# Fourteen places of their own for the second token weights' tiles, and an earlier start of their loads, in a spectral filter followed by an MLP mixer

## The chip, the cores and the metric

The kernel runs on one core of a Trainium2 chip. The metric is the device time of one execution in microseconds (us), as the median of several runs. The engines are named as in the profile: PE is TensorE (PEld its weight loads), DVE is VectorE, ACT is ScalarE, POOL is GpSimd and SP is SyncE. SP, ACT and POOL also issue DMAs, each in the order of its own instructions; all of them are carried by the same 16 DMA engines.

## The reference

The input has 8 batches of 3008 positions and 256 channels. A spectral filter is applied along the positions, and then an MLP mixer whose first half mixes positions ("token") and whose second half mixes channels:

```
X = np.fft.rfft(x, axis=1)
x = np.fft.irfft(X * (filt_r + 1j * filt_i)[None], n=3008, axis=1)
h = np.maximum(x.transpose(0, 2, 1) @ w_tok1, 0.0) @ w_tok2     # w_tok1 3008x256, w_tok2 256x3008
u = x + h.transpose(0, 2, 1)
out = u + np.maximum(u @ w_ch1, 0.0) @ w_ch2                    # w_ch1 256x1536, w_ch2 1536x256
```

The four mixer weights arrive as 64-bit floats. [...]

## The kernel before

**Two parts.** An opening (up to about 170 us) filters batch 0 and loads and converts all weights; then `mix` walks over 8 batches x 6 column blocks x 6 pairs of channel groups, and the filter of the next batch (`dft` of the next group) is spread between its items.

**The filter of batch 0.** `dft(GROUPS[0])` first transforms 12 pieces of x (`a_unit`, L534) and leaves the result, turned by DVE, in the tile `turned`. Then come 32 steps k. A step has a PE product with the table (`b_unit`, L666: it reads `turned[:, k, :]`), a DVE product with the filter (L671), the PE products back (`bi_unit`, L680), and an ACT copy (L690); after every second step ACT issues a DMA that writes the copies to a DRAM tensor, `g_tmp` (L687). In the same loop POOL loads the filter's rows for later steps (`filt_load`, six DMAs per two steps, L243 to L251), SP loads table pieces (L583), and ACT copies filter rows to the tile's other half (L255). In the last steps and behind the loop, `t4_load` reads `g_tmp` back in another layout (L782): rows of steps 0 to 15 first, then 16 to 23, then 24 to 27, and last those of steps 28 to 31 (six DMAs, three from SP and three from POOL). With these last rows `token_sums` can start (L788, 48 PE products), and then `token_relu` (L864) and the first parts of u (`u_part`, L882 and L874).

**The weights.** A tile of 64-bit weights is brought in and converted in four stages, written as a generator: `begin` issues the DMA into a staging place; `copy` is an ACT instruction that takes the upper words (L283); `middle` is two DVE instructions (L285, L286); `end` is two more (L289, L291), and then either two PE products that add the halves, with an ACT copy out (L329, L330, L332), or DVE additions (L318). The list `tiles` fixes the order: 12 tiles of w_tok1 (`w1_tile`, loaded by SP), 14 of w_tok2 (`w2_load`, L362, loaded by POOL, 470 KB each but 188 KB for the last of each half; the first six go the PE way, the others the DVE way), two of w_ch1 (`wc1_load`, L394, four DMAs of 128 KB each), and the ten of `LAST` (w_ch1 and w_ch2, L394 and L405). Conversion goes at a fixed place of the program: one half tile (a `middle` or an `end`) per filter step, then one tile after another behind the loop, between the token sums and the parts of u, and the rest in the first items of `mix`. For channel tiles POOL forms sums of the weights (`combine`, L382 to L386).

**Where a tile waits and when it is begun.** `stages` lists, in the order of the tiles, the pool and tag of the staging place: 12 times the pool t4, then sixteen places that go round over the two buffers each of u, t and v, then t2 and t3 in turn. So the seventh tile of w_tok2 takes the place of the first one and its DMA waits until DVE has read that. `fill` begins tiles as long as fewer than 5 (for the tiles of `LAST`, 4) lie between the begun and the ended ones; it runs at the end of every conversion, not in the last five filter steps (`pause`), and once more behind the loop, ahead of the last `t4_load`s. `ended` counts program order: a DMA is placed in POOL's queue there, and the queue then goes on by its own waits.

**The region that is shared.** The pool `wcp` has one buffer. Before `mix`, it holds `turned` (columns 0 to 8191 of 32-bit words, 256 for each step) and a small table `wa0` (128 columns more), which is read only by `a_unit`. Behind the filter's loop the same buffer becomes `both`, the channel weights (`chan`, 10,752 columns). The first write into it is the addition L318 of the first channel tile.

Of the kernel before, what the change touches and what calls it, by code (L numbers as in the profile page):

```python
# [10 lines left out]
FP32 = mybir.dt.float32  # L11
I64 = mybir.dt.int64
# [7 lines left out]
N1 = 47  # L20
N2 = 64
NF = N // 2 + 1
D = 256
P = 128
K2 = 32
A = 24
# [14 lines left out]
TC = DT // P  # L41
DC = 1536
JT = DC // P
JP = JT // 2
DH = D // P
# [3 lines left out]
NG = 10  # L49
W2G = -(-N2 // NG)  # L50
# [80 lines left out]
def kernel(  # L131
# [31 lines left out]
    def pool(name, bufs, **kw):  # L163
        return ctx.enter_context(tc.tile_pool(name=name, bufs=bufs, **kw))

    glob = pool("glob", 1)
    wcp = pool("wcp", 1)
# [6 lines left out]
    t4p = pool("t4p", A // TC4 + 1)  # L174
# [36 lines left out]

    w2m = [w2[:, t, 0:7 * 256].rearrange("p (s n) -> p s n", s=7) for t in range(2)]

    turned = wcp.tile([P, K2 * D + P], FP32, tag="wc", name="turned")
    wa0 = turned[:, K2 * D:]
    turned = turned[:, 0:K2 * D].rearrange("p (s d) -> p s d", d=D)
    chan = []


# [46 lines left out]

    early = [(up, "u")] * 2 + [(tp, "t")] * 2 + [(vp, "v")] * 2
    late = [(t2p, "t2"), (t3p, "t3")]
    stages = [(t4p, "t4")] * (A // 2) + (early * 3)[0:TC * W2G + DH] + late * 5

    def stage(n):
        where, tag = stages.pop(0)
        return where.tile([P, n], I64, tag=tag, name="st")

    def halves(st, n, pair):
# [45 lines left out]
    ended = [0]  # L321
# [14 lines left out]
    def w1_tile(i):  # L336
        st = stage(512)
        rows = moe_w_tok1.rearrange("(n2 n1) t -> n2 n1 t", n1=N1)
        q = nc.sync if i < EARLY else nc.gpsimd
        if 2 * i + 2 == A:  # L340
            nc.gpsimd.memset(st.bitcast(U32)[:, 512:1024], 0)
        for j in range(2):
            a = 2 * i + j
            both = a + 1 < A
            src = bass.AP(tensor=rows.tensor, offset=rows.offset + (A - 1 - a) * DT,
                          ap=[[N1 * DT, N2]] + [[(1 + 2 * a) * DT, 2]] * both + [[1, DT]])
            q.dma_start(st[0:P:1 if both else 2, ts(j, DT)], src)
        yield

        h = halves(st, 512, spare_pair())  # L350
        yield next(h)
        yield next(h)
        on_chip(wai_t, *next(h), 512, [(lambda v: v, w1[:, 2 * i:2 * i + 2, :].rearrange("p a t -> p (a t)"))])

    def w2_load(i):

        t, g = divmod(i, W2G)
        nn = min(NG, N2 - g * NG)
        n = nn * N1

        st = stage(512)
        nc.gpsimd.dma_start(st[:, 0:n], moe_w_tok2[ts(t, P), ds(g * NG * N1, n)])  # L362
        yield
        dst = w2[:, t].rearrange("p (a h n2) -> p h n2 a", h=2, n2=HALF)[:, :, ds(g * NG, nn), :]

        def some(h, first, step, w):
            return (lambda v: bass.AP(tensor=v.tensor, offset=v.offset + first, ap=[v.ap[0], [N1, nn], [step, w]]),
                    dst[:, h, :, 0:w])

        parts = [some(0, A - 1, -1, A), some(1, A, 1, A - 1)]  # L370
        if i < BY_PE:
            h = halves(st, n, spare_pair())
            yield next(h)
            yield next(h)
            on_chip(ident, *next(h), n, parts)
        else:
            yield from rounded(st, n, parts, False)
# [12 lines left out]
    def wc1_load(i, late=True):  # L390
        c, q = divmod(i, DC // 512)
        st = stage(512)
        for g in range(CB):
            nc.gpsimd.dma_start(st[ts(g, CW)], moe_w_ch1[ds((g * DH + c) * CW, CW), ts(q, 512)])  # L394
        yield

        yield from rounded(st, 512, [(lambda v: v.rearrange("p (i j n) -> p i j n", j=2, n=P),
                           chan[0][:, 2 * q:2 * q + 2, slice(0, 5, 4) if c == 0 else slice(1, 7, 5)])], late)
        if c == DH - 1 and 2 * q >= PLAIN:
            combine(chan[0][:, 2 * q:2 * q + 1])  # L400
            put_off.append(2 * q + 1)

    def wc2_load(i):
# [11 lines left out]
        while put_off:  # L415
# [4 lines left out]
    LAST = ((wc2_load, 0), (wc1_load, 1), (wc1_load, 4), (wc2_load, 1), (wc1_load, 2), (wc2_load, 2), (wc1_load, 5),  # L420
            (wc2_load, 3), (wc2_load, 4), (wc2_load, 5))

    tiles = ([w1_tile(i) for i in range(A // 2)] + [w2_load(i) for i in range(TC * W2G)]
             + [wc1_load(c * (DC // 512), False) for c in range(DH)] + [f(i) for f, i in LAST])
# [20 lines left out]
    def convert_end(copy_now=True):  # L445
        ended[0] += 1
        advance(end)
        if copy_now:
            copies()
        fill(5)  # L450
# [9 lines left out]
    begun, pause = [0], []  # L460

    def fill(ahead):
        while not pause and begun[0] < len(tiles) and begun[0] < ended[0] + (4 if begun[0] >= len(tiles) - len(LAST) else ahead):
            start()

    def start():
        advance(begin)
        begun[0] += 1
# [3 lines left out]
    xs, ahead = {}, []  # L472
# [304 lines left out]
    t4 = {}  # L777
# [481 lines left out]
    with tc.manual_schedule():  # L1259
# [36 lines left out]
        pause.clear()  # L1296

        fill(5)
        for c in range(A // TC4):
            t4_load(0, c, PARTS[3], P, (nc.sync, nc.gpsimd)[c % 2])  # L1300
# [27 lines left out]
        n = MT * JP  # L1328
# [58 lines left out]
```

## Time and profile before

| what | value |
|---|---|
| runs shown | 2398.6, 2398.96, 2395.35 us (median 2398.6) |
| the profiled execution | 2395.43 us, its span from first to last instruction 2393.7 us |
| TensorE's granted clock | 0.996 of full speed over the span |
| PE busy 0 to 100 / 100 to 200 / 200 to 300 / 300 to 400 us | 82.52 / 93.88 / 96.20 / 100.00 us |
| the filter's steps | L666 begins at 31.44 us, the last L680 ends at about 102.7 us |
| last write of g_tmp (L687), and POOL's read behind it (L782) | issued at 104.39 us and 108.88 us |
| token sums (L788) | begin at 111.00 us |
| DMAs of w_tok2 (L362) | fourteen, issued from 65.1 to 113.7 us; to landing 4.1 / 6.9 / 10.1 us (least, median, most) |
| DMA over the span | 294.28 MB, 123 GB/s on average; 210 to 283 GB/s between 60 and 106 us |

A row of a timeline has the start, the duration, the engine, the line, the operation with its output and input, and in brackets the idle time before it with what ended it. A row of waits has the engine, its line and tile, what it waited for, and then the total in us, the number of times and the longest. A row of stretches has the stretch and its length, each engine's busy time with the number of instructions, the granted clock, the busy share of the DMA engines and what they moved in GB/s; since transfers overlap, the share can be over 1.

### The profile page before, as it was taken

To read this page: it belongs to the slowest core of one execution; us is meant where nothing else is said; L and a number is where in the kernel's file an instruction comes from. 1 tells how busy PE (TensorE), PEld (TensorE's weight loads), DVE (VectorE), ACT (ScalarE), POOL (GpSimd) and SP (SyncE) were. 2 spreads that over 40 slices of the span, in tenths; PEclk is the share of its full clock that TensorE was granted. 3 is DMA by queue.
4 is the path that set the end of the run, shared out by engine and by line. 5 is a ranking of instruction groups with operands and counts; after the bars stand their busy time and mean duration, and the time that the engine had idled before them with its cause. 6 is when DMAs were issued, how large, how long until landed. Compare 5 with 4: busy or idle time off the path is not lost.

```text
span 2393.7 us, 36991 instructions
## 1 busy us (share of the span) xinstructions
PE 2356.6 (98%) x13108; PEld 2007.5 (84%) x13108; DVE 1943.6 (81%) x3653; ACT 688.1 (29%) x1339; POOL 641.0 (27%) x1124
## 2 busy tenths in 40 slices
PE   7999999999999999999999999999999999999998
PEld 4667789888898888988888888988889888898887
DVE  7797887888887888878887788788888788877776
ACT  5732222322223222232222222132222322212222
POOL 8485533211211121222111211221121112112121
PEclk8999999999999999999999999999999999999999
DMA  8864446333354333533344333533335433331100
GB/s 228 235 197 134 146 129 223 112 108 94 112 178 134 94 96 110 198 112 95 104 154 153 107 94 104 193 113 108 94 112 177 135 94 97 108 130 33 38 15 21
DMA packets 190423, 294.28 MB, mean 123 GB/s; under 512 B 34444, under 2 KB 124962, under 8 KB 190238
## 3 DMA queue, kind: packets, MB, share of 16 engines
q1 hardware_dynamic: 148750, 231.24, 31.1%
q0 software_dynamic: 34688, 53.83, 8.6%
q10 hardware_dynamic: 6800, 6.85, 0.9%
q8 instruction: 104, 1.70, 0.3%
q14 instruction: 81, 0.66, 0.1%
HBM read 209.06 MB, written 82.72 MB: 122 GB/s over the span
## 4 chain that ended last, share of the span: by engine, by line
PE 93%; DVE 3%; DMA 2%; issue 1%; POOL 1%; ACT 0%; SPq 0%; DVEq 0%; ACTq 0%; POOLq 0%
PE ps_po L1022 35%; PE ps_pg L975 20%; PE ps_pg L1004 15%; PE ps_b L527 3%; PE ps_b L839 3%; PE ps_acc L896 3%; PE ps_pg L527 2%; PE ps_acc L839 2%; PE ps_b L896 2%; PE ps_acc L874 2%; PE ps_b L874 2%; DVE t L953 1%; PE ps_pg L666 1%; DMA x<-in_x_dram 1%; PE ps_b L680 1%
## 5 line engine op out<-in xcount | busy, mean ns | idle before, releaser
L1030 POOL DMA_DIRECT2D out_dram<-r x752 | 408.3, 551 | 1452.1 <-issue 864.0
L1009 ACT ACTIVATE hh<-hh 128x512 f32<-128x512 f32 (+1 forms) x568 | 342.7, 621 | 989.1 <-DVE hh L953 989.1
L953 DVE TENSOR_TENSOR hh<-ps_pg,s 128x512 f32<-128x512 f32 (+3 forms) x852 | 475.4, 585 | 167.2 <-ACT s L978 157.1
L1022 PE MATMUL ps_po<-t,wc 128*128 128x256 f32 (+1 forms) x2296 | 556.4, 379 | 0.8 <-DVE t L953 0.8
L1022 PEld LDWEIGHTS ps_po<-t,wc 128*128 128x128 f32 x2296 | 427.1, 190 | 93.0 <-issue 33.9
L1022 PE MATMUL ps_po<-hh,wc 128*128 128x256 f32 (+1 forms) x1722 | 411.5, 375 | 1.1 <-POOL wc L386 1.1
L975 PE MATMUL ps_pg<-v,wc 128*128 128x256 f32 (+1 forms) x1704 | 406.6, 375 | 0.0
L1022 PEld LDWEIGHTS ps_po<-hh,wc 128*128 128x128 f32 x1722 | 326.8, 190 | 40.2 <-POOL wc L386 1.9
L975 PEld LDWEIGHTS ps_pg<-v,wc 128*128 128x128 f32 x1704 | 323.5, 190 | 36.9 <-DVE v L953 0.4
L1004 PE MATMUL ps_pg<-u,wc 128*128 128x256 f32 (+1 forms) x1136 | 287.7, 376 | 3.3 <-DVE hh L953 3.1
L953 DVE TENSOR_TENSOR t<-t,hh 128x256 f32<-128x256 f32 (+1 forms) x576 | 247.6, 430 | 19.8
L1004 PEld LDWEIGHTS ps_pg<-u,wc 128*128 128x128 f32 x1136 | 213.9, 190 | 32.7 <-DVE hh L953 7.5
L953 DVE TENSOR_TENSOR s<-ps_pg,hh 128x512 f32<-128x512 f32 (+1 forms) x284 | 193.3, 681 | 29.6
L978 ACT COPY s<-ps_pg 128x256 f32<-128x256 f32 (+1 forms) x284 | 104.4, 367 | 326.5 <-PE ps_pg L975 326.4
L953 DVE TENSOR_TENSOR t<-hh 128x512 f32<-128x512 f32 (+1 forms) x288 | 194.4, 675 | 0.6 <-ACT hh L1009 0.6
L975 PE MATMUL ps_pg<-u,wc 128*128 128x256 f32 (+1 forms) x568 | 166.9, 375 | 0.4 <-DVE hh L953 0.4
L1004 PE MATMUL ps_pg<-v,wc 128*128 128x256 f32 (+1 forms) x568 | 166.4, 375 | 0.0
L975 PEld LDWEIGHTS ps_pg<-u,wc 128*128 128x128 f32 x568 | 106.3, 190 | 14.1 <-DVE hh L953 2.1
L1004 PEld LDWEIGHTS ps_pg<-v,wc 128*128 128x128 f32 x568 | 107.3, 190 | 12.7
L953 DVE TENSOR_TENSOR u<-ps_acc,u 128x256 f32<-128x256 f32 (+1 forms) x84 | 46.1, 549 | 72.4 <-PE ps_acc L896 50.2
L953 DVE TENSOR_TENSOR u<-ps_b,u 128x512 f32<-128x512 f32 (+2 forms) x126 | 74.5, 591 | 28.9 <-PE ps_b L896 26.7
L896 PE MATMUL ps_acc<-w 128*128 128x256 f32 (+1 forms) x336 | 85.2, 376 | 0.0
(168 smaller groups left out, 2708.4 us busy)
## 6 DMA issues: line engine op xcount, KB each, us to landing
w<-w_tmp SPq DMA_DIRECT2D x84, 448.0 KB
w<-w_tmp SPq DMA_DIRECT2D x35, 896.0 KB
out_dram<-r POOLq DMA_DIRECT2D x696, 32.0 KB, 3.5
g_tmp<-t SPq DMA_DIRECT2D x112, 192.0 KB
t<-g_tmp SPq DMA_DIRECT2D x42, 512.0 KB
t<-z_tmp SPq DMA_DIRECT2D x196, 96.0 KB
z_tmp<-t SPq DMA_DIRECT2D x72, 256.0 KB
wb<-wbi_t SPq DMA_DIRECT2D x56, 256.0 KB
```

Of the source, the lines that this page charges most:

```text
L527: nc.tensor.matmul(outs(i, j), stat(i, j), mov(i, j), start=True, stop=True)
L666: nc.tensor.matmul(ps, wbs[k // WC][:, 0:2 * P:2, k % WC], turned[:, k, :].unsqueeze(1), start=True, stop=True)
L839: nc.tensor.matmul(ps[:, at], w[:, n], mov, start=(j == 0 and i in (0, 2)), stop=(j == AP - 1 and i >= 5))
L874: nc.tensor.matmul(ps[:, ds(q * P, n)], t4[b, c][:, r, ts(dh, P)], wai[:, 0:n], start=(first and q == 0), stop=(not first and q == 3))
L896: nc.tensor.matmul(ps[:, ds(j * hw, hw)], h1[:, n, :], w2m[m % 2][:, at, 0:hw], start=(i < 2 and j == 0), stop=(j == len(todo) - 1))
L953: nc.vector.tensor_tensor(out=out, in0=in0, in1=in1, op=op)
L975: nc.tensor.matmul(ps[:, 0:hw], chan[0][:, jp, n, :], mov, start=True, stop=True)
L978: nc.scalar.copy(out=s[:, 0], in_=g[0][:, 0, 0:hw])
L1004: nc.tensor.matmul(ps[:, 0:hw], chan[0][:, jp, n, :], mov, start=True, stop=True)
L1009: nc.scalar.activation(out=hs, in_=hs, func=AF.Relu)
L1022: nc.tensor.matmul(po[i][:, j, 0:hw], chan[1][:, jp, n, :], mov, start=(jp == 0 and first == 1), stop=(jp == JP - 1 and last == 1))
L1030: q.dma_start(bass.AP(tensor=ob.tensor, offset=ob.offset + row * D + g * cw, ap=[[N1 * D, 32], [D if h else -D, n], [1, cw]]), blocks[ts(g ...
```

## The change

The buffer of `wcp` gets the name `early_wc` and its full width from the start. Twelve w_tok1 tiles keep their places. The fourteen w_tok2 tiles get a place each: the six buffers of u, t and v; three behind `wa0` (from column 8320 on, 940 columns apart); and five in the columns of `turned` (0, 1024, 2048, 3072, 4096; each the columns of four steps). An exchange in the list gives the narrow last tile of the first half the last, short piece. The two first w_ch1 tiles take the buffers of u (before: of t). From the twelfth tile on, `fill` may run 5 tiles ahead of the ended ones and one more for every two tiles ended beyond two, up to 11; the tiles of `LAST` stay at 4. The order of the conversions is the same.

```diff
-    turned = wcp.tile([P, K2 * D + P], FP32, tag="wc", name="turned")
-    wa0 = turned[:, K2 * D:]
-    turned = turned[:, 0:K2 * D].rearrange("p (s d) -> p s d", d=D)
+    early_wc = wcp.tile([P, 2 * JP * 7 * P], FP32, tag="wc", name="turned")
+    wa0 = early_wc[:, K2 * D:K2 * D + P]
+    turned = early_wc[:, 0:K2 * D].rearrange("p (s d) -> p s d", d=D)
...
-    stages = [(t4p, "t4")] * (A // 2) + (early * 3)[0:TC * W2G + DH] + late * 5
+    stages = [(t4p, "t4")] * (A // 2) + early + [(early_wc, K2 * D + P + n * NG * N1) for n in (0, 2, 4)]
+    stages += [(early_wc, n * 4 * D) for n in range(5)] + early[0:DH] + late * 5
+    stages[A // 2 + W2G - 1], stages[A // 2 + 8] = stages[A // 2 + 8], stages[A // 2 + W2G - 1]
 
     def stage(n):
         where, tag = stages.pop(0)
+        if where is early_wc:
+            return where[:, ds(tag, min(2 * n, 2 * JP * 7 * P - tag))].bitcast(I64)
         return where.tile([P, n], I64, tag=tag, name="st")
...
     def fill(ahead):
-        while not pause and begun[0] < len(tiles) and begun[0] < ended[0] + (4 if begun[0] >= len(tiles) - len(LAST) else ahead):
+        while not pause and begun[0] < len(tiles):
+            if begun[0] >= len(tiles) - len(LAST):
+                ahead = 4
+            elif begun[0] >= A // 2:
+                ahead = 5 + min(max(ended[0] - 2, 0) // 2, 6)
+            if begun[0] >= ended[0] + ahead:
+                break
             start()
```

## The prediction

> **What bounds the kernel now.** I read the engines' busy time first, then TensorE's waits, then tables of stretches over the start.
>
> The page's first part:
>
> ```profile
> PE 2356.6 (98%) x13108; PEld 2007.5 (84%) x13108; DVE 1943.6 (81%) x3653; ACT 688.1 (29%) x1339; POOL 641.0 (27%) x1124
> ```
>
> TensorE (PE) is idle for only 2393.7 - 2356.6 = 37 us. The table in steps of 100 us puts 17.5 us of it before 100 us, 6.1 between 100 and 200, 3.8 between 200 and 300, and almost none from there to 2300 us. So the bound is TensorE, and only the opening can move: a microsecond won or lost before about 260 us moves the end by a microsecond. The change acts between 60 and 170 us. TensorE's waits from 111 us to 262 us:
>
> ```profile
> PE ps_pg L1004 <- DVE hh L953: 3.1, 3, 2.7
> PE ps_b L788 <- DMA t<-g_tmp: 2.1, 1, 2.1
> PE ps_po L1022 <- POOL wc L386: 1.1, 2, 0.6
> PE ps_po L1022 <- DVE t L953: 0.8, 3, 0.4
> PE ps_acc L882 <- ACT h L864: 0.7, 1, 0.7
> PE ps_pg L975 <- DVE hh L953: 0.4, 1, 0.4
> ```
>
> No row names the weight loads that the change moves. The second does matter: L788, the first batch's token sums, starts at 111.00 us, when the filter's result has been written to DRAM (g_tmp) and read back. Next, who waited between 96 and 131 us:
>
> ```profile
> POOL t L782 <- DMA g_tmp<-t: 10.1, 1, 10.1
> ...
> ACT both L283 <- DMA st<-in_moe_w_tok_dram: 6.4, 2, 5.6
> ```
>
> ScalarE (ACT) waits 5.6 us for a second-token-weight load (call these tiles w2 0 to 13), because GpSimd's (POOL's) queue held five of them for 10.1 us behind the reads of g_tmp. VectorE (DVE) then waits too; from its timeline:
>
> ```profile
> 116.59 0.41 DVE L285 TENSOR_SCALAR both<-both 128x470 uint32<-128x470 uint32 x1 [2.46 <-ACT both L283]
> ```
>
> Last, the stretches; the last two columns are the busy share of the 16 DMA engines and GB/s:
>
> ```profile
> 60.00:70.00 10.00, 10.00 (x40) 7.75 (x39) 7.90 (x15) 8.84 (x16) 8.90 (x17) 1.00 0.72 210
> 70.00:80.00 10.00, 10.00 (x39) 7.73 (x39) 7.76 (x15) 8.86 (x17) 8.12 (x16) 1.00 0.87 238
> 80.00:90.00 10.00, 10.00 (x36) 7.16 (x35) 6.95 (x13) 9.01 (x16) 4.48 (x9) 1.00 1.05 239
> 90.00:98.00 8.00, 7.97 (x31) 6.23 (x30) 6.13 (x12) 7.10 (x15) 0.54 (x1) 1.00 0.87 283
> 98.00:106.00 8.00, 6.61 (x21) 3.66 (x19) 5.97 (x12) 6.21 (x14) 0.54 (x1) 1.00 0.97 232
> 106.00:110.00 4.00, 2.63 (x6) 1.00 (x6) 2.88 (x8) 2.44 (x6) 1.02 (x3) 1.00 0.28 83
> ```
>
> The DMA engines are nearly full from 60 to 106 us and then almost free for 4 us. In those 4 us the last write of g_tmp (issued at 104.39, landed at 108.30) and its first read (108.37 to 110.86) take place.
>
> **The change part by part.**
>
> *What it moves.* Before, w2 0 to 5 are issued from 65.1 to 85.7 us, w2 6, 7 and 8 at 89.3, 93.5 and 98.3 (each waiting for its place), w2 9 to 13 from 110.6 to 113.7 and the first channel tile at 119.2 to 123.5. After, all fourteen have places that need no wait: u, t, v and the tail of the region are free, and its columns are read for the last time by step 19, before 75 us. By the new allowance two loads come at step 13 (about 61 us) and eleven by step 25; the last three and the channel tile (into u, free at 88.7 us) follow at once. All stand ahead of POOL's reads of g_tmp.
>
> *Issue.* Each load costs POOL the same 0.55 us as before. Five come earlier within the filter's loop, and POOL idles 0.5 to 0.7 us per two steps there, so I cost them at nothing; the filter's loads behind them are needed 15 us later by step count and land in 2 to 7.5 us. If that cover fails, ACT's copy L255 waits.
>
> *The gain.* VectorE's 2.46 us go. Its conversions run one after another at 2.94 us (starts at 119.53, 122.51, 125.44), so all later ones come up to 2.46 us earlier, until VectorE meets what TensorE paces: v at 140.91 needs ACT's u (done at 138.75, lead 2.1), t at 150.09 needs hh (done at about 149.2, lead 0.9). A lead of 0.9 removes TensorE's 0.16 at 150.8 and 0.55 at 158.1, and most of 0.57 at 167.1, whose POOL L386 follows VectorE's L318: 0.9 to 1.3, I take 1.1. Ends: 0 (a later load is late instead) and 2.5 (the whole lead). The 2.7 us at 210.9 stay: they end a chain of DMAs from TensorE's own unit at 183.6, which moves along.
>
> *The cost.* The loads keep their bytes; they now lie ahead of the transfers that start L788. What one occupies: the five issued at 110.55 to 112.19 and 113.66 land 5.3, 6.2, 7.5, 10.1 and 9.5 us later; the first and third are (119.15 - 115.85) / 2 = 1.65 us apart per 470 KB. Pulled ahead of 106 us are four such (6.6), the 188 KB one (0.66) and 512 KB of channel weights (1.8): 9.1 us of DMA time. Free before 106 us by the table: 2.8 + 1.3 + 0 + 1.0 + 0.2 = 5.4 us (one minus the share, times the length). If all of it can be filled, 9.1 - 5.4 = 3.7 us are left when the last write is issued; if half, 6.4. Transfers land about in the order in which they were issued, whichever queue they came by: w2 8, issued on POOL's queue at 98.27, takes 8.5 us to 106.8, and reads of 64 KB issued by SyncE (SP) at 99.1 and 99.7 land at 107.0 and 107.2. So what is left delays the last write, its read and L788. No trace of before has this load at this place: ends 0 and 6.4, and I take 5.0, the middle of 3.7 and 6.4.
>
> A rule speaks against that order. The Trainium skill (DMA: Bandwidth & Descriptors, Queues, rings and completion order) says that each DMA engine takes the queues in turn, packet by packet, so that SP's reads would not stand behind POOL's backlog. The landings at 107 us do not show it. By the rule the sum would be about 0 (second rival).
>
> *Places shared with a live tile.* The filter's steps 20 to 31 still read the region's other columns. Waits go by the columns touched: TensorE's second unit loads weights from this tile at 6.03 us, while the first unit's copy into other columns runs only at 7.12. So nothing (third rival otherwise).
>
> *Sum.* +5.0 - 1.1 = +3.9 us on the profiled execution's 2395.43, that is 2399.3. The runs shown spread: 2395.35, 2398.6 and 2398.96, and with the profiled one their mean is 2397.1. I predict 2397.1 + 3.9 = 2401.0. A measurement of this kernel tells 0.2% (4.8 us) from no change, so this lies within it.
>
> **The rivals.**
>
> *ACT is held too (slower).* ACT's write of steps 28 and 29 was ready at 101.2 us and issued at 102.01: the copy behind it waits 1.2 us for a read of g_tmp, issued by SP at 97.1, to land (101.9), since they share a completion semaphore. If such reads land 10 us after issue, as w2 5 did (85.67, 9.7 us), that is 107: ACT stalls about 5 us, and the last steps' copies and the last write follow it. Then the write is issued near 109.4, and 3.9 + 2.5 us of write and read come on top: L788 near 117.4, +6.4, net +5.3 or 2402.4. It decides once the reads of 96.3 to 98.5 land later than about 104. For it: the 9.7 us, and 8.1 us for the read of 98.53. Against: POOL itself is held by its own semaphores at 80 to 86 us (waits of 0.3 to 0.9), which thins its backlog.
>
> *The queues share.* If each queue gets its turn at the engines, the last write and first read wait only about as long again as they occupy them: between 95 and 111 us queue q10 takes 14.6% of 16 us for three writes (0.8 each), q1 34.8% for eighteen transfers (0.3): 1.1 us. With the gain: 0, or 2397.1. Against: the landings at 107 us. (This is where the rule above would lead.) If moreover w2 8's absence after 98 us frees ACT's 1.2 us and VectorE's lead counts whole, -3.7, or 2393.4.
>
> *Waits go by the whole tile.* Then step 24's matmul (about 84 us) waits for w2 9, loaded just before it: 10 us, as the 9.7 above, so 2407. Against: 6.03 before 7.12.
>
> *The change doesn't bring the loads forward*, because POOL is held. Then 0, as for sharing queues.
>
> **How the numbers follow.** Forecast 0.48; ACT held 0.27; queues share, or loads not forward 0.17; gain only 0.05; whole tile 0.03. Slower by over 0.2% (+4.8): all of the whole tile, three quarters of ACT held (0.20), a quarter of the forecast, whose own span is 3.7 - 1.1 to 6.4 - 1.1, or +2.6 to +5.3 (0.12): 0.35. Faster by over 0.2% needs more than the gain rival offers, but for the spread of runs: 0.05. The rest, 0.60, is within. The range goes from 2393.5 (gain only) to 2405.0 (ACT held at 2402.4, with the runs' own 1.9 above their mean); the whole tile is left out.
>
> **What would show it.** Gain: ACT's 5.6 us wait for w2 and VectorE's 2.46 are gone, and POOL L386 no longer holds TensorE at 158 and 167. Cost: L788 starts near 116 us, not 111.0; the DMA share between 106 and 110 us is near 1; w2 loads issued about 90 us land more than 8 us later. ACT held: its wait for a read of g_tmp is well over 1.2 us. If L788 starts at or before 111 us, my order of landings or the free time is wrong, and the kernel is up to a few us faster; if TensorE waits in the filter's loop (L666, L680), a cover failed and it is slower than I say.

## The result and the profile after

The changed kernel takes 2403.7 us (median of 9 runs, 2401.68 to 2406.36), the kernel before, beside it, 2396.42 us (9 runs, 2394.95 to 2398.96). The ratio is 1.0032, with an interval of 1.0023 to 1.004: slower by 7.3 us. The profiled execution took 2404.92 us with a span of 2403.1, which is 9.4 us more than the span before. The change made the kernel slower, as forecast, and the time lies in the forecast range (2393.5 to 2405.0), but above the forecast of 2401.0: +3.9 us was forecast, and slower by more than 0.2% (4.8 us) had a chance of 0.35.

Busy time, the page's first part, of the kernel after:

```profile
PE 2361.8 (98%) x13108; PEld 2011.7 (84%) x13108; DVE 1943.0 (81%) x3653; ACT 688.7 (29%) x1339; POOL 641.6 (27%) x1124
```

TensorE has the same 13108 matmuls, but is busy 5.2 us longer with them. It is no new work, so its matmuls were slower somewhere. The rest of the 9.4 us, 4.2, is idle time. TensorE's waits from 111 to 271 us:

```profile
PE ps_b L798 <- DMA t<-g_tmp: 5.2, 1, 5.2
PE ps_pg L1014 <- DVE hh L963: 3.8, 2, 2.8
PE ps_po L334 <- DVE both L295: 2.9, 1, 2.9
PE ps_acc L892 <- ACT h L874: 0.7, 1, 0.7
PE ps_po L1032 <- DVE t L963: 0.4, 1, 0.4
PE ps_po L1032 <- POOL wc L390: 0.4, 1, 0.4
```

Lines behind the change have moved by 10 (L788 is L798, L687 is L697), those of the conversion by 4 (L330 is L334, L283 is L287); in the kernels built on experiment 1 below, lines behind the change have moved by 4 as well (L788 is L792). The wait of the token sums has grown from 2.1 to 5.2 us, and a wait of L334, a matmul ahead of them, has come in. The waits for POOL's sums went from 1.1 to 0.4; the forecast had them nearly gone. The stretches (the columns are as before: busy time of PE, PEld, DVE, ACT and POOL, the granted clock, the DMA share, GB/s), first two of the kernel before, then the kernel after:

```profile
110.00:120.00 10.00, 9.01 (x42) 7.98 (x43) 7.23 (x18) 1.90 (x4) 3.94 (x8) 1.00 1.03 281
120.00:130.00 10.00, 10.00 (x48) 8.81 (x47) 9.66 (x21) 2.05 (x4) 7.22 (x15) 1.00 0.63 189
```

```profile
60.00:70.00 10.00, 10.00 (x38) 7.49 (x37) 8.19 (x15) 9.03 (x17) 7.85 (x14) 1.00 0.92 266
...
106.00:110.00 4.00, 1.90 (x5) 0.68 (x4) 0.90 (x3) 1.70 (x5) 0.00 (x0) 1.00 0.96 283
110.00:120.00 10.00, 3.70 (x8) 2.49 (x9) 9.14 (x23) 3.52 (x8) 2.87 (x6) 0.61 0.66 151
120.00:130.00 10.00, 10.00 (x42) 8.58 (x41) 9.62 (x22) 2.02 (x4) 7.79 (x16) 0.87 0.93 236
```

From 106 to 110 us the DMA engines are now 0.96 busy, where they were 0.28. And the clock column, 1.00 in these stretches before, is 0.61 and 0.87: TensorE ran at half its clock from 112.27 to 122.51 us.

To account for the 9.4 us I took the start of every matmul in both traces and subtracted. The difference is 0.8 us from 37 us on, before the change acts; 6.36 at the start of the token sums (117.36 against 111.00); 8.90 at 122.6, once the half clock is over; 7.48 at 175; 9.01 at 222, after a second stretch of half clock (218.08 to 221.50); the spans differ by 9.4. So four terms: later token sums +6.4, half clock behind them +2.5, the lead that VectorE gains -1.4, a second half clock +1.5; 0.4 is left over. The forecast had the first and the third.

### The profile page after: what moved, and what is told of

It is laid out like the page before. It is cut to its first block, busy times and chain, and to the rows that moved or that the text cites. A ratio compares the mean times of both kernels' runs of the same rounds, so it can differ in the third digit from the quotient of the medians.

```text
span 2403.1 us, 36980 instructions
## 1 busy us (share of the span) xinstructions
PE 2361.8 (98%) x13108; PEld 2011.7 (84%) x13108; DVE 1943.0 (81%) x3653; ACT 688.7 (29%) x1339; POOL 641.6 (27%) x1124
## 4 chain that ended last, share of the span: by engine, by line
PE 92%; DMA 3%; DVE 2%; POOL 1%; issue 1%; ACT 1%; SPq 0%; DVEq 0%; ACTq 0%; POOLq 0%
PE ps_po L1032 34%; PE ps_pg L985 19%; PE ps_pg L1014 15%; PE ps_b L537 3%; PE ps_b L849 3%; PE ps_acc L906 3%; PE ps_pg L537 2%; PE ps_acc L849 2%; PE ps_b L906 2%; PE ps_acc L884 2%; PE ps_b L884 2%; PE ps_b L798 1%; DMA filt<-in_filt_i_dram 1%; DMA g_tmp<-t 1%; DMA x<-in_x_dram 1%
```

## The experiments

Each was timed over five rounds beside the kernel before; the difference of medians is against that kernel's median in the same set of runs (2395.14 us for experiments 1 to 4, 2395.21 for 5 to 8 and 2394.79 for 9 to 12).

**1. The places alone.** `fill` is put back as it was; `stages` stays as changed.

```diff
-        while not pause and begun[0] < len(tiles):
-            if begun[0] >= len(tiles) - len(LAST):
-                ahead = 4
-            elif begun[0] >= A // 2:
-                ahead = 5 + min(max(ended[0] - 2, 0) // 2, 6)
-            if begun[0] >= ended[0] + ahead:
-                break
-            start()
+        while not pause and begun[0] < len(tiles) and begun[0] < ended[0] + (4 if begun[0] >= len(tiles) - len(LAST) else ahead):
+            start()
```

> The changed kernel's fourteen places with the old allowance (five begun ahead, in the loop too), so that the last loads are again issued behind the reads of g_tmp. If the cost lies in the loads being begun early (my theory), this is the kernel before: token sums start at 111 +- 0.7 us, no half clock near 112 us, 2396.4 +- 1 us. If the places themselves cost (the region shared with live columns, rival), a matmul of the filter's loop waits and 3 us or more of the 7.3 us are found here: 2400 us or above.

2395.37 us, +0.2 (ratio 1.0, 0.9991 to 1.0008). Token sums at 109.80 us. The places cost nothing; the earlier start does. (The token sums are even 1.2 us earlier than before. Without a wait for their places, loads 6 to 8 go out at 87.1 to 88.5 us, where they went out at 89.3 to 98.3; that this is the reason was not tested.)

**2. Spare matmuls in the waits of the changed kernel.**

```diff
+            if spare_matmuls:
+                extra = bank(turn[1])
+                for _ in range(spare_matmuls):
+                    nc.tensor.matmul(extra, wa, w1_all[:, 0:512], start=True, stop=True)
             nc.tensor.matmul(ps[:, 0:n], stat, rest, start=False, stop=True)
...
-            on_chip(ident, *next(h), n, parts)
+            on_chip(ident, *next(h), n, parts, 3 if i == BY_PE - 1 else 0)
...
-        acc = bank(free_bank()).rearrange("p (t d) -> p t d", t=TC)
+        full = bank(free_bank())
+        for _ in range(6 if b == 0 else 0):
+            nc.tensor.matmul(full[:, 0:512], wa, w1_all[:, 0:512], start=True, stop=True)
+        acc = full.rearrange("p (t d) -> p t d", t=TC)
```

> The changed kernel with nine spare matmuls of 512 columns (0.86 us each) in TensorE's two long waits: three ahead of the last tile matmul that waits for VectorE at 108 us, six ahead of the token sums. They compute nothing that is used. If the half clock from 112.3 to 122.5 us is the price of the waits (theory), the clock stays at 1.00 there, the token sums still start near 117.4 us but their first 24 matmuls take as long as in the kernel before, and the time falls by 2.4 us, from 2403.7 to 2401.3 (the stretch near 218 us may stay). If the half clock has another cause (rival), it stays, and the time is 2403.7 or above.

2399.31 us, +4.2 (ratio 1.0019, 1.0011 to 1.0028), where the changed kernel is at +7.3 and, run again, at +9.3. Two stretches of each, after first, then this kernel:

```profile
104.00:112.00 8.00, 4.76 (x12) 1.66 (x10) 4.76 (x11) 2.89 (x8) 0.00 (x0) 1.00 0.85 256
112.00:123.00 11.00, 5.84 (x16) 4.60 (x16) 10.11 (x25) 3.55 (x7) 5.86 (x12) 0.53 0.79 172
```

```profile
104.00:112.00 8.00, 7.62 (x19) 3.28 (x18) 4.79 (x14) 3.91 (x10) 0.00 (x0) 1.00 0.88 256
112.00:123.00 11.00, 11.00 (x44) 8.16 (x43) 10.59 (x23) 2.38 (x4) 6.14 (x12) 1.00 0.83 178
```

The clock stays at 1.00, and matmuls that compute nothing make the kernel some 3 us or more faster. Nothing was wrong with the token sums' matmuls; the idle time ahead of them slowed them. That is more than the 2.4 expected, but two more things differ in this execution: the token sums begin at 115.47, not 117.36, and there is no second half clock (the wait of 2.8 us ahead of it is 1.1 here).

**3. Less data in the loads pulled ahead.** The issues stay; loads 9 to 13 carry a tenth, so most of these weights are left out.

```diff
-        nc.gpsimd.dma_start(st[:, 0:n], moe_w_tok2[ts(t, P), ds(g * NG * N1, n)])
+        some_n = n if i < 9 else n // 10
+        nc.gpsimd.dma_start(st[:, 0:some_n], moe_w_tok2[ts(t, P), ds(g * NG * N1, some_n)])
```

> The changed kernel, its order of issue untouched, but second-token-weight loads 9 to 13 bring only a tenth of their columns (the rest of those tiles is left as it was, so that part of the token weights is not loaded). If the cost is the DMA time that lies ahead of g_tmp's last write and read (theory), 6.8 us of it are gone: ScalarE is not held, token sums start at 111 to 112 us, the clock stays at 1.00 there, and only the gain is left: 2395.3 us, 1.1 below the kernel before. If the cost comes from the issues, the places or the waits on POOL's queue (rival), the token sums stay near 117 us and the time near 2403.7.

2398.92 us, +3.8, and wide: 2393.97 to 2401.45. Four of the eleven runs lie at 2395.4 or below, as the theory has it; the others do not, nor does the profiled execution (2400.43), whose token sums start at 115.08. The theory missed a second cost. In this execution the filter's loop itself is late, before any of the small loads matters: the matmul at 95.18 us (98.72 here) comes 3.5 us later than before. The next experiment shows the same, and more plainly.

**4. Ten early, four behind the reads.**

```diff
-        while not pause and begun[0] < len(tiles):
+        while not pause and begun[0] < min(len(tiles), hold[0]):
...
         for c in range(A // TC4):
             t4_load(0, c, PARTS[3], P, (nc.sync, nc.gpsimd)[c % 2])
+        hold[0] = len(tiles)
+        fill(5)
```

Here `hold` starts at `[A // 2 + 10]`.

> The changed kernel, but only ten of the fourteen second-token-weight tiles are begun in the filter's loop; the last four and the first channel tile are begun behind the last reads of g_tmp, as before. Theory: load 10 lands where load 9 did (about 115.8 us) and is needed 2.94 us later, so VectorE's 2.46 us are gone; what is pulled ahead is one load of 1.65 us and load 8 some us earlier, which fits into the 5.4 us that were free: token sums at 111 to 112.5 us, no half clock; the time is 0 to 1.1 us below the kernel before, 2395.3 to 2396.4. If any load pulled ahead costs its full time (rival), token sums start at 113 us or later and the time is 2398 or above.

2394.24 us, -0.9 (ratio 1.0, 0.9991 to 1.0009); six of the eleven runs lie at 2393.6 to 2394.3, five at 2395.9 to 2400.3. The profiled one (2399.67) is of the latter. What POOL, VectorE and TensorE waited for in it, ahead of the token sums:

```profile
POOL st L366 <- DMA st<-in_moe_w_tok_dram: 4.1, 2, 3.0
POOL turned L366 <- DMA st<-in_moe_w_tok_dram: 2.8, 2, 1.7
```

```profile
DVE p L681 <- ACT filt L255: 6.1, 6, 1.4
DVE p L681 <- DMA filt<-in_filt_i_dram: 4.9, 1, 4.9
```

```profile
PE ps_b L690 <- DVE p L681: 3.3, 1, 3.3
```

Read from the top: POOL, about to issue a weight load (L366), waits up to 3.0 us for an older weight load to land. The filter loads behind it in POOL's queue are issued later, the last of them from 94.66 to 98.15 us where the first profile of the changed kernel has 87.74 to 92.11. So VectorE waits 4.9 us for one, and TensorE 3.3. Why POOL waits can be read from the semaphores: its DMAs take eight in turn (99 to 106 in the trace), and an issue waits until the DMA that had that semaphore last has landed. A pair of filter steps has six filter loads. With one weight load that makes seven, and each load meets another semaphore every time; with two it makes eight, and each weight load waits for the weight load of one pair of steps earlier, which takes 7.5 to 8.6 us to land (62.31 to 69.80, 62.87 to 71.49), while a pair lasts about 4.4 (the kernel before issues its filter loads at 61.83, 66.20, 70.61). That the semaphores cause the whole delay is not shown: the hold of 2.4 us just ahead of 94.66 waited for the older load (landed at 94.07), but also for VectorE (94.07) and ScalarE (94.21), and this trace cannot separate them.

**5 to 7. The dose.** From the kernel of experiment 1, with 1, 3 or 5 loads begun behind the filter's loop in place of none, and nothing changed inside it. POOL runs ahead of TensorE, so it issues them already at 89 to 96 us.

```diff
-        fill(5)
+        fill(6)
         for c in range(A // TC4):
             t4_load(0, c, PARTS[3], P, (nc.sync, nc.gpsimd)[c % 2])
```

The other two have `fill(8)` and `fill(10)`.

> The kernel with the new places and the old allowance (e1_places), and one load more (tile 9) begun right behind the filter's loop, ahead of the last reads of g_tmp. Landings in order of issue (theory): 1.65 us more lie ahead of the last write, of which the engines had 1.2 us free between 98 and 106 us: token sums 0 to 1 us later than in e1_places; ScalarE's and VectorE's waits for tile 9 are gone, worth 0.9 to 1.3 us: 2394.3 to 2395.2 us, at or up to 1 us below the kernel before. Queues in turn (rival): token sums not later at all, 2394 us.

> As e5_one, with three loads (tiles 9 to 11) ahead of the last reads. In order of issue (theory): 5.0 us of loads, 1.2 to 1.8 free: token sums 3 to 4 us later than in e1_places, less the gain of 1.1, and perhaps a half clock (1 to 2.4 us): 2397 to 2400 us. Queues in turn (rival): token sums at most 1 us later, 2394 to 2395 us.

> As e5_one, with all five loads (tiles 9 to 13) ahead of the last reads, and none of them inside the loop. In order of issue (theory): 7.3 us of loads, 1.2 to 1.8 free: token sums 5.5 to 6.5 us later than in e1_places, ScalarE not held in the loop since the reads that it shares a semaphore with were issued before; a half clock of 2.4 us; less the gain: 2401 to 2403.5 us, about the changed kernel's time, so that the early issue in the loop adds nothing of its own. Queues in turn (rival): 2394 to 2395.5 us.

| loads behind the loop | token sums start at | median, us | against before | ratio |
|---|---|---|---|---|
| none (experiment 1) | 109.80 | 2395.37 | +0.2 | 0.9991 to 1.0008 |
| one | 109.55 | 2392.66 | -2.6 | 0.9981 to 0.9998 |
| three | 114.70 | 2398.24 | +3.0 | 1.0001 to 1.0019 |
| five | 114.75 | 2399.06 | +3.9 | 1.0006 to 1.0024 |

One load fits in the free DMA time and beats both kernels; its gain, 2.6, is larger than the 1 us at most that was expected. Three of TensorE's waits in it from 104 to 262 us; the last of them, for POOL's sums of weights, was 1.6 in experiment 1 and 1.1 before:

```profile
PE ps_po L334 <- DVE both L295: 1.0, 1, 1.0
...
PE ps_b L792 <- DMA t<-g_tmp: 0.6, 1, 0.6
PE ps_po L1026 <- POOL wc L390: 0.4, 1, 0.4
```

The spans of experiments 1 and 5 differ by 1.9 us, of which that wait explains 1.2; the rest I do not assign. With three loads it turns at once. So the queues do not share evenly: that rival wanted about 2394 to 2395.5 for all three. Three and five cost nearly the same, which simple order of issue did not foresee (3 to 4 and 5.5 to 6.5 us), and ScalarE was held after all. Its timeline with five loads ("ACTq" is its queue, issuing the write of `g_tmp`):

```profile
101.22 0.36 ACT L694 COPY t<-ps_acc 96x256 f32<-96x256 f32 x1
105.85 0.31 ACTq L691 DMA_DIRECT2D g_tmp<-t  x1
106.20 0.95 ACT L336 COPY w<-ps_po 128x240 f32<-128x240 f32 x2 [4.61 <-DMA t<-g_tmp]
```

The copy is done at 101.6, the write goes out at 105.85: it waits for its semaphore, last used by a read of `g_tmp` that SP issued at 97.36 and that landed at 105.77. Behind it in ScalarE's order stand L336 and L287, the copy that VectorE needs for the next tile, and TensorE waits 4.54 us for that tile (L334). By the time it gets to the token sums, at 114.75, their first read has landed (114.61 here, 113.44 with three loads). So in these two kernels the path runs through the held ScalarE. With five loads the read comes only 0.14 us ahead, and its own chain hangs on ScalarE too: the last write went out at 108.56, where the kernel before had it at 104.39.

**8. Spare matmuls again, ahead of the token sums alone, with five loads.** The second part of experiment 2's edit, with 8 in place of 6, on experiment 7's kernel.

> As e7_five, with eight spare matmuls of 512 columns (0.86 us each, unused) on TensorE ahead of the token sums. If the wait itself halves the clock (theory), the clock stays at 1.00 from 38 us to beyond 130 us and the time is 2 to 2.5 us below e7_five; the token sums start within 0.5 us of where they do there. If the clock has nothing to do with the wait (rival), the time is that of e7_five or above.

2403.83 us, 4.8 above experiment 7. The expectation missed, for the reason just found: the wait is at L334, a few matmuls earlier. The clock was already halved there, the token sums did not wait, and the spare matmuls (116.06 to 122.92) cost their own time.

**9 to 11. Other semaphores for the last writes.** The reads of rows 96 to 111 are dropped from the loop and joined to those of rows 112 to 127 behind it. With six DMAs fewer in the common order of SP and ScalarE, the last two writes follow older reads on their semaphores. Applied to experiments 5 and 7 and to the changed kernel.

```diff
-                elif k in (30, 31):
-                    for c in range(3):
-                        t4_load(0, 3 * (k - 30) + c, PARTS[2], PARTS[3])
...
-            t4_load(0, c, PARTS[3], P, (nc.sync, nc.gpsimd)[c % 2])
+            t4_load(0, c, PARTS[2], P, (nc.sync, nc.gpsimd)[c % 2])
```

> e5_one with the reads of g_tmp's rows 96 to 111 and 112 to 127 made one read per tile, issued behind the loop (six reads fewer). The last two writes of g_tmp then share their completion semaphores with reads issued 1 to 2 us earlier than before. If a shared semaphore is what holds ScalarE (theory), its waits of about 1.1 us ahead of the last L336 copies go; the last reads have twice the rows, which costs 0 to 1.5 us: 2392 to 2393.5 us. If it is not (rival), the waits stay and only the longer reads count: 2393 to 2394.5 us.

> e7_five with the same merged reads. The last two writes then share semaphores with reads that landed at 102.3 and 104.2 us in e7_five, in place of 105.8 and 108.5. If the shared semaphore holds ScalarE (theory), the two writes are issued near 102.4 and 104.4 us, its waits of 4.6 and 0.8 us go, TensorE's wait of 4.5 us for L334 goes, and TensorE waits for the reads of g_tmp instead, since the last write still lands behind the five loads at about 110: token sums at 112.5 to 113.5 us (114.75 in e7_five), time 1 to 2.5 us below e7_five: 2396.5 to 2398. If ScalarE is held by something else (rival), the waits stay and the time is 2399 or above.

> The changed kernel with the merged reads. ScalarE's wait of 3.8 us at 107.9 goes, the last write is issued near 104.4 us and not 107.9; it lands behind the loads at 112 to 112.5, and the first merged read right after it: token sums at 115 to 115.5 us, not 117.4. Theory (order of issue decides, the semaphore adds about 2 us): 1.5 to 2.5 us below the changed kernel. If the semaphore were the whole cost (rival), token sums would be back at 111 to 112 us and the time 6 us below the changed kernel.

One load: 2393.62 us, -1.2 (ratio 0.9987 to 1.0004). ScalarE's wait of 1.07 us ahead of L336 at 102 us is gone (0.38 is left), but nothing is won over experiment 5 (2392.66); the intervals overlap, and which of the two is better stays open. This execution has a half clock at 208.84 to 212.26 us, and that of experiment 5 has none there. Five loads: 2397.14 us, +2.4 (ratio 1.0003 to 1.0021), where experiment 7 had +3.9, token sums at 112.44. The same rows as above in this kernel:

```profile
101.88 0.34 ACT L694 COPY t<-ps_acc 96x256 f32<-96x256 f32 x1
104.05 0.31 ACTq L691 DMA_DIRECT2D g_tmp<-t  x1
104.41 0.96 ACT L336 COPY w<-ps_po 128x240 f32<-128x240 f32 x2 [2.18 <-DMA t<-g_tmp]
```

The write now waits for a read that landed at 103.98, and goes out at 104.05: the semaphore it is, though 2.2 of the 4.6 us stay, and TensorE still waits for L334 (2.1 us), not for the reads as expected. The changed kernel with merged reads: 2402.7 us, +7.9, beside +9.3 for the changed kernel in the same set (ratios 1.0019 to 1.0044 and 1.0023 to 1.0048, so the 1.4 between them is not clear of noise), token sums at 115.24. ScalarE is not held in it at all, and TensorE still waits 5.18 us for the read. So the semaphore is not the whole cost: the last write, issued at 105.37, takes 7.1 us to land (112.50), where the kernel before has 3.9, and the read follows it.

**12. The changed kernel once more.**

> The changed kernel once more, beside the others on the same chip: by its first runs 1.0023 to 1.004 of the kernel before, 2400.7 to 2404.8 us. Its profile shows whether the half clock after the token sums' wait comes again (theory: it does, since the wait is longer than one 3.4 us period of the clock) and the one near 218 us (which by theory depends on where the period's edges fall, so it may be absent), and whether a filter load comes late in the loop, as in the profiles of e3_small_loads and e4_ten_early.

2404.1 us, ratio 1.0036 (1.0023 to 1.0048). TensorE's waits from 60 to 300 us in its profile:

```profile
PE ps_b L798 <- DMA t<-g_tmp: 6.0, 1, 6.0
PE ps_pg L1014 <- DVE hh L963: 3.1, 3, 2.6
PE ps_b L690 <- DVE p L681: 1.7, 1, 1.7
```

Here ScalarE is not held (the last write goes out at 105.72, not 107.94), and yet the write lands no earlier: at 113.65, where it was 113.52. In both executions SP's read behind it goes out at 114.01, a moment after an earlier read with the same semaphore has landed (113.99). So the hold of ScalarE moved the token sums of the changed kernel little, if at all. But in this execution a filter load is late, and TensorE waits 1.7 us in the loop. POOL's longest wait before it:

```profile
POOL st L366 <- DMA st<-in_moe_w_tok_dram: 6.0, 2, 5.2
```

The token sums start at 116.43, 5.44 us later than before. The clock is halved for two periods behind the wait (+2.2), VectorE's lead gives back 1.4, and the half clock near 218 us is there again (+1.3); 8.1 at the last matmuls.

## Why the prediction was right, and where its size was wrong

**The step that failed is the sum.** It was written as "+5.0 - 1.1 = +3.9": one cost, one gain. Both terms are there at nearly that size, but a third was missing. That the time still fell into the range is in part luck: the forecast's own span ended at +5.3, that is 2402.4, and the range reached further only by the spread of the runs. (By its own terms, 2402.4 + 1.9, it ends at 2404.3 and not at 2405.0; the 2403.7 lies below both.)

*The clock, not in the sum: +3.5 to +4.0 us.* The prediction priced the wait of L788 by its length alone. In each profile of the changed kernel TensorE stands nearly idle from 108.3 to 117.4 (or 110.4 to 116.4) us, its granted clock falls to 0.50, and it returns to 1.00 only after one full period of work: 10.24 us of half clock in one, 6.83 in the other, both multiples of 3.41. Experiment 2 removes it. The Trainium skill (TensorE: Matmul & The Clock Gate, Part 1) says that the clock is halved after an idle window of about 3.4 us, and that the windows run freely, whatever the kernel does. The traces agree on the length and on the free run, but show that a window need not be quite idle. The windows also explain the stretch near 218 us. The kernel before has a wait of 2.67 us there too (208.18 to 210.85). Counted in steps of 3.41 us from the end of the opening's half clock at 34.89, a window's edge at 208.97 splits it, 45% of the worse window is work, and the clock stays. In the changed kernel 2.4 us of a wait of 2.83 lie in one window (214.67 to 218.08), with 29% of work, and the clock falls for 3.41 us (the first row is the kernel before):

```profile
210.85 1.13 PE L1004 MATMUL ps_pg<-u,wc 128*128 128x256 f32 x4 [2.67 <-DVE hh L953]
...
214.21 1.46 PE L1032 MATMUL ps_po<-hh,wc 128*128 128x256 f32 x6
218.49 2.08 PE L1014 MATMUL ps_pg<-u,wc 128*128 128x256 f32 x4 [2.83 <-DVE hh L963]
220.36 1.06 PE L1014 MATMUL ps_pg<-v,wc 128*128 128x256 f32 x2
```

The four matmuls at 218.49 take 1.87 us (to 220.36), in the kernel before 0.96. So that cost hangs on where the windows fall, and is not the change's alone. Counted in this way over all fourteen traces, from 40 to 2370 us, every window at full clock with at most 41% of work was followed by the half clock, and none with 49% or more was; with 45% one was (experiment 11, from 108.52 us) and one was not (the kernel before).

*The delay of L788: +5.0 forecast, +6.4 and +5.4 measured.* The order of landings came as read. The write of `g_tmp` that ScalarE issued at 97.43 landed at 110.64, between POOL's loads of 96.13 (110.42) and 96.66 (111.01); in experiment 12, 98.27 to 108.92, between those of 98.12 and 98.65. SP waits for that write before it reads the rows back, here from 96 to 120 us, first in the kernel before and then in the kernel after:

```profile
SPq L782 <- DMA g_tmp<-t: 5.3, 2, 4.4
...
SPq L792 <- DMA g_tmp<-t: 8.9, 2, 8.7
```

Of the 1.4 us beyond 5.0 in the first profile, 0.8 was there at 37 us. The rule that was weighed against this order, that DMA engines take the queues in turn (the Trainium skill, DMA: Bandwidth & Descriptors, Queues, rings and completion order), did not help the write, though the packets show something of it: between 101 and 107 us the engines moved 1.10 MB of POOL's queue, 0.49 of SP's and 0.17 of ScalarE's side by side. So the transfers do not simply go one behind the other; but the write's first packet started 4.3 us after its issue (101.75), and its last byte landed among loads that had been issued with it. What sets this pace is not shown. The same section also says that the increment of a completion semaphore lands only after every earlier write of its DMA engine, across its queues; the landings agree with that sentence.

*The gain: -1.1 forecast, -1.4 measured in both profiles.* It is won where the prediction said: the difference to the kernel before falls near 151, 158 and 167 us of that kernel. In the changed kernel alone this would not prove VectorE's lead, since TensorE comes there 8.9 us late and so waits less in any case. Experiment 5 does: its TensorE is 1.4 us early, and wins 1.4 more at the same places (from -1.44 to -2.85). Without the cost, places and one early load together are worth 2.6.

*"Issue at nothing": half wrong.* The cover, POOL's idle time, was real, but not the limit: POOL was held by its own eight semaphores, to a degree that differs between executions. TensorE lost next to nothing in the loop in the first profile, 1.7 us in experiment 12, 3.3 in experiment 4. The prediction had named the sign to look for, a wait of L680.

*The rivals.* "ACT is held too" met its condition in the first profile: the read issued at 97.07 landed at 107.87, later than 104; ScalarE waited 3.8 us; and the token sums started at 117.36, where it said 117.4. That agreement is luck: its own terms, 109.4 + 3.9 + 2.5, give 115.8, no more than the forecast; and the write went out earlier, at 107.94, but it and the read behind it took longer (5.6 and 3.2 us from issue to landing). In experiments 11 and 12 ScalarE is not held, and the token sums are only 2.1 and 0.9 us earlier; so it is shown on the path only where the loads come behind the loop (experiments 6 and 7). "The queues share" fell with experiments 6 and 7 as far as it said that a small transfer hardly waits, "waits go by the whole tile" with experiment 1. "Gain only" was right for one load in place of five.

## What to carry to other kernels

A load pulled ahead costs what it displaces: before a prefetch, look whose transfer is issued next, and count the free DMA time up to it. Here 1.65 us fitted and won 2.6, and 5.0 us lost 3.0. Price a longer wait of TensorE by its length and by the half clock behind it (here 2.2 to 2.5 us more). And where DMAs take completion semaphores in turn, count how many are issued until the same one comes round again, on each engine that shares them.

## What the runs showed that was not expected

- A window of 3.41 us halved TensorE's clock wherever at most 41% of it was work, and left it wherever 49% or more was. It came back behind windows with 86 to 100% of work; up to 89%, in the openings of some runs, was not enough.
- Eight DMAs per pair of steps on eight semaphores made POOL wait up to 5.2 us for a load to land; with seven it waited at most 0.9 (kernel before).
- A DMA that waits for its semaphore holds its engine's compute: ScalarE stood idle for 4.6 us, and the copy behind the DMA, whose input was ready at 104.7 us, ran at 106.2 (experiment 7).
